# Retention and a multiplicative FFN: loads of two attention units moved ahead of weight pieces, four weight pieces converted one at a time, and the fifth unit's products moved ahead of a block's second step

## The chip, the cores and the metric

The kernel runs on one core of a Trainium2 chip. The core has five engines that take their instructions in order, each from its own queue: TensorE (PE, matrix products and transposes), VectorE (DVE), ScalarE (ACT), GpSimd (POOL) and SyncE (SP, which here only issues transfers). Transfers run on 16 DMA engines beside them. The metric is the time of one execution on the device in microseconds (us), lower is better.

## The reference

```python
# q, k, v: (B, H, S, D) = (8, 8, 576, 64)
scores = scale * np.matmul(q, k.transpose(0, 1, 3, 2))
Dmat = np.where(rel >= 0, gamma[:, None, None] ** rel[None, :, :], 0.0)
ret = scores * Dmat[None, :, :, :]
attn = np.matmul(ret, v)
x = attn.transpose(0, 2, 1, 3).reshape(B * S, H * D)   # 4608 tokens x 512
a = x @ w1                                             # 512 x 1024
b = x @ w2                                             # 512 x 1024
h = a * b @ w3                                         # 1024 x 1024
out = h @ w_out                                        # 1024 x 512
```

The attention is a causal product of scores with a decay that depends on the head and on the distance of the two positions. Its output is the input of a feed-forward part, in which two products of x are multiplied element by element. `w3` and `w_out` are multiplied with each other first, since nothing stands between them. q, k and v are float32. The four weights are float64, and the kernel turns them into float32 itself.

## The kernel before, in words

**Attention in units.** Two batches and 64 or 128 positions make a unit. The 576 positions of the first pair of batches are units 0 (64 positions) to 4 (128 each). The later pairs follow much later and are not touched by the change. One unit `g` goes through these steps:

- `load(g, names)` (L138 to L147): SP issues one transfer per name. Each is 512 KB (256 KB for unit 0). Two buffers per name hold the units, so unit 2's k waits until unit 0's k is no longer read.
- `scale(g, "q")` and `scale(g, "v")` (L256 to L266): multiply by the decay. v goes to POOL (L265), q to DVE (L265) for units 0 and 1, and to ACT in eight instructions (L263) for later ones; unit 4's v goes to ACT also.
- `front(g, "k")` or `"q"` (L268 to L283): 8 transposes on PE into two PSUM banks (L279), and two copies on ACT (L282).
- `score(g)` (L285 to L300): 16 products (L294) into four banks, then four maskings on DVE into `pm` (L297).
- `state(g)` (L302 to L322): the running k-v state: 16 products (L317) and a copy on ACT (L321).
- `pv_state(g)` and `pv(g)` (L326 to L380): products of the state with q (L336) and of the masked scores with v (L363) in two banks. The function that `pv` returns copies the result into the token tiles `xT` on ACT (L370).

**Weights in pieces.** `load_block` (L395) has SP issue one piece of 512 KB of a float64 weight, as one transfer (L406) or two (L409). There are five buffers, `raw`. `conversion` (L500) turns a piece into float32: `begin_block` gets the exponent `e` and the mantissa `m`, `end_block` puts sign and exponent together (L474) and multiplies (L485). The exponent comes from ACT in three instructions (L456, L457, L458), or, for the numbers listed in L450, from DVE in one (L452) and ACT in two (L454, L458). DVE makes the mantissa (L460, L463). `conversion` is a generator that goes forward one step for each `convert(1)`. The list in L506 holds the pieces at which the next one is not begun before the one at hand is ended. Pieces 0 to 3 are the first quarter of w1 and w2; each later four make the next quarter.

**The up products.** A block of tokens has 384 rows: 192 of each of two batches. `plain(0, 0, 0, w)` (L625) multiplies the first block with the first quarter of w1 (w=0) or w2 (w=1), in 16 products (L638) whose first eight need one piece and whose last eight the next. For w=0, ACT copies the result (L643). For w=1, DVE multiplies it in (L645). All later steps are `up(i, n, fp)` (L567), by Strassen's scheme: seven groups of four products (L585), sums of weights (`strassen_weights`, L203), sums of tokens (`strassen_tokens`, L556), five additions on DVE (L590), copies on ACT (L598, L613) and a multiplication (L619). Between them, `convert` steps and functions from the list `aside` are placed. `up(0, 1, 0)` is the second block's first step, `up(0, 0, 1)` the first block's second.

**What sets the order.** It is written out by hand, from L815 on: each engine runs its part of this program in the order in which it is written. PSUM banks for all this are seven (`acc`), handed out in turn. `keep_busy(n)` (L181) puts `n` products without use on PE.

Of the kernel before, what the change touches and what calls it, by code (L numbers as in the profile page):

```python
# [42 lines left out]
def kernel(  # L43
# [13 lines left out]
    nc = tc.nc  # L57
# [80 lines left out]
    def load(g, names, engine=nc.sync, tag=None):  # L138
        i, c = divmod(g, NC)
        sz = sizes[c]  # L140
        src = {"k": k, "q": q, "v": v}
        for nm in names:
            t = pools["ld"].tile([P, 2 * H, D], F32, tag=tag or "ld_" + nm, name="ld_" + nm,
                                 bufs=3 if tag else 2 if g < NC else 1)
            engine.dma_start(
                t[:sz], src[nm][2 * i:2 * i + 2, :, starts[c]:starts[c] + sz, :].rearrange("b h p d -> p (b h) d"))
            live[nm, g] = t  # L147
# [33 lines left out]
    def keep_busy(n):  # L181

        t = acc.tile([P, P], F32, tag="acc", name="idle")
        for _ in range(n):
            nc.tensor.matmul(t, ident, ident, start=True, stop=True)
# [70 lines left out]
    def scale(g, nm, scalar=False, engine=nc.gpsimd):  # L256
        c = g % NC
        sz = sizes[c]
        t, gam = live[nm, g], {"q": gq, "v": gk}[nm]
        t = t[:sz].rearrange("p (b h) d -> p b h d", b=2)  # L260
        if scalar:
            for h in range(H):
                nc.scalar.mul(t[:, :, h, :], t[:, :, h, :], gam[:sz, c, h:h + 1])  # L263
            return
        engine.tensor_tensor(  # L265
            out=t, in0=t, in1=gam[:sz, c].unsqueeze(1).unsqueeze(3).to_broadcast([sz, 2, H, D]), op=ALU.mult)  # L266

    def front(g, names="kq"):  # L268
        c = g % NC
        sz = sizes[c]  # L270
        for nm in names:
            src = live[nm, g]
            dst = pools["fr"].tile([P, 2, NP, P], F32, tag=nm + "T", name=nm + "T",
                                   bufs=1 if nm == "k" and g >= NC else 2)
            for b in range(2):
                tp = acc.tile([P, NP, P], F32, tag="acc", name="tp")
                for p in range(NP):
                    h = b * H + 2 * p
                    nc.tensor.transpose(tp[:, p, :sz],  # L279
                                        src[:sz, h:h + 2, :].rearrange("p a d -> p (a d)"),  # L280
                                        ident[:sz, :sz])
                nc.scalar.copy(dst[:, b, :, :sz], tp[:, :, :sz])  # L282
            live[nm + "T", g] = dst  # L283
# [18 lines left out]
    def state(g):  # L302
        c = g % NC
        sz = sizes[c]
        if c == NC - 1:
            return
        vs = live["v", g]
        kn = live["k", g]
        if c == 0:
            live["st"] = st_ps.tile([P, 2, NP, D], F32, tag="st", name="st")  # L310
        st = live["st"]

        for b in range(2):
            for p in range(NP):
                for j, hs in enumerate(heads):
                    h = b * H + 2 * p + j
                    nc.tensor.matmul(st[hs, b, p, :], kn[:sz, h, :], vs[:sz, h, :],  # L317
                                     start=(c == 0 and b == 0 and p == 0), stop=(c == NC - 2),
                                     skip_group_check=True)
        sb = pools["fr"].tile([P, 2, NP, D], F32, tag="sb", name="sb", bufs=2 if g < NC else 1)  # L320
        nc.scalar.copy(sb, st)  # L321
        live["sb", g + 1] = sb  # L322
# [72 lines left out]
    def load_block():  # L395
        n = loaded[0]
        if n == len(blocks):
            return
        key, w = blocks[n]
        t = raw.tile([P, CV, 2], I32, tag="raw", name="raw", bufs=5)  # L400
        if key[0] == "w12":
            _, fp, _, r = key
            t2 = t.rearrange("p (c n) t -> p c n t", c=2)
            src = w[2 * r * P:2 * (r + 1) * P, fp * QC:(fp + 1) * QC]
            if r == 0:
                nc.sync.dma_start(t2, src.rearrange("(c p) n t -> p c n t", p=P))  # L406
            else:
                for half in range(2):
                    nc.sync.dma_start(t2[heads[half]],  # L409
                                      src.rearrange("(c a d) n t -> a d c n t", a=2, d=D)[1 - half])  # L410
        elif key[0] == "wo":
            src = w.rearrange("(a i x) n t -> i a x n t", i=KF, x=BL)[key[1]]
            for a in range(QP):
                nc.sync.dma_start(t[a * BL:(a + 1) * BL], src[a])
        else:
            _, ft, h = key
            src = w[ft * P:(ft + 1) * P].rearrange("(j r) (a h f) t -> h a r j f t", r=BL, a=QP, h=DF // CV)
            for a in range(QP):
                nc.sync.dma_start(t[a * BL:(a + 1) * BL].rearrange("p (j f) t -> p j f t", j=P // BL), src[h, a])
        live["raw", n] = t  # L420
        loaded[0] += 1
# [13 lines left out]
    def begin_block():  # L435
        n = begun[0]
        t = live["raw", n]
        lo, hi = t[:, :, 0], t[:, :, 1]
        top = t.rearrange("p n t -> p (n t)").bitcast(BF16).rearrange("p (n u) -> p n u", u=4)[:, :, 3]
        e = raw.tile([P, CV], I32, tag="exp", name="e")  # L440
        m = raw.tile([P, CV], I32, tag="man", name="m")
        vec = nc.vector

        half = e.bitcast(BF16).rearrange("p (n u) -> p n u", u=2)[:, :, 1]
        func = mybir.ActivationFunctionType
        if n in (1, 2, 3, 2 * NQ - 1):  # L450

            vec.tensor_scalar(out=e, in0=hi, scalar1=1, scalar2=21,  # L452
                              op0=ALU.logical_shift_left, op1=ALU.logical_shift_right)
            nc.scalar.activation(e, e, func.Relu, bias=lim[:, 0:1], scale=-1.0)  # L454
        else:
            nc.scalar.activation(half, top, func.Abs)  # L456
            nc.scalar.activation(e, half.bitcast(U16), func.Relu, bias=lim[:, 0:1], scale=-1.0 / 16.0)  # L457
        nc.scalar.activation(e, e, func.Relu, bias=lim[:, 1:2], scale=-2.0 ** 23)  # L458

        vec.tensor_scalar(out=m, in0=hi, scalar1=0x000FFFFF, scalar2=0x00100000,  # L460
                          op0=ALU.bitwise_and, op1=ALU.bitwise_or)
        yield
        vec.scalar_tensor_tensor(m.bitcast(F32), in0=lo.bitcast(U32), scalar=2.0 ** -32, in1=m,  # L463
                                 op0=ALU.mult, op1=ALU.add)
        live["em", n] = e, m
        begun[0] += 1
        yield
# [32 lines left out]
    def conversion():  # L500

        yield from begin_block()
        while converted[0] < len(blocks):
            if begun[0] < len(blocks) and converted[0] not in (0, 3, 4, 6, 7):  # L506
                yield from begin_block()
            yield from end_block()
            if begun[0] == converted[0] < len(blocks):
                yield from begin_block()  # L510
# [11 lines left out]
    def convert(n):  # L522

        for _ in range(n):
            if go_on() is not None:
                return
# [286 lines left out]


    load(0, "v")  # L815
    load(1, "kq")
    load_block()
    load(1, "v")
    for _ in range(3):
        load_block()  # L820
    scale(0, "q", engine=nc.vector)
    front(0, "k")
# [1 line left out]
    front(0, "q")  # L824
    score(0)
    scale(0, "v")
    state(0)
    front(1, "k")
    pv(0)()
    scale(1, "q", engine=nc.vector)  # L830
    load(2, "kqv")
    load_block()
    keep_busy(3)
    front(1, "q")
    convert(2)
    score(1)
    scale(1, "v")
    pv_state(1)
    convert_up_to(1)
    pv(1)()  # L840
    convert(2)
    state(1)
    load(3, "kqv")
    convert_up_to(2)
    load_block()
    convert_up_to(3)
    load_block()
    plain(0, 0, 0, 0)
    front(2, "k")
    convert_up_to(4)  # L850
    load_block()
    plain(0, 0, 0, 1)
    scale(2, "q", True)
    scale(2, "v")
    front(2, "q")
    convert(2)
    score(2)
    convert_up_to(5)
    state(2)
    load(4, "kq")  # L860
    scale(3, "q", True)
    list(strassen_weights(0))
    front(3, "k")
    copies = pv(2)
    scale(3, "v")
    copies()
    front(3, "q")
    load(4, "v")
    list(strassen_tokens(0, 0, nc.vector))
    state(3)  # L870
    score(3)
    pv(3)()
    list(strassen_tokens(0, 1, nc.vector))
    convert_up_to(6)
    aside.extend([lambda: scale(4, "q", True), lambda: None, lambda: front(4, "k"), lambda: front(4, "q")])
    up(0, 1, 0, conv=2, tail=False)
    owed.append(2)
    while ("S", 1) not in live:
        convert(1)
    score(4)  # L880
    aside.append(lambda: scale(4, "v", True))
    up(0, 0, 1, conv=2, tail=False)
    owed.append(2)
    pv(4)()
    up(0, 1, 1, conv=[2, 1, 0, 2, 2], tail=False)
    owed.append(2)
    up(0, 0, 2, conv=[2, 1, 1, 2, 2], tail=False)
# [509 lines left out]
```

## Time and profile before

| What | Value |
|---|---|
| median of 3 runs | 819.23 us (818.91 to 821.7) |
| the profiled execution | 820.0 us |
| its span | 818.3 us |
| granted clock, mean of the span | 0.998 |
| DMA | 115.34 MB, mean 141 GB/s |

The stretches of 20 us show where the engines are busy. The columns are the stretch, its length, then PE, PEld (weight loads of PE), DVE, ACT and POOL busy with the number of instructions, the granted clock, the busy share of a DMA engine, and GB/s.

```profile
0.00:20.00 20.00, 16.91 (x239) 15.28 (x239) 7.95 (x18) 8.08 (x15) 3.17 (x9) 1.00 1.04 179
20.00:40.00 20.00, 18.05 (x161) 17.44 (x163) 13.13 (x21) 11.53 (x24) 3.47 (x2) 0.91 1.07 210
40.00:60.00 20.00, 19.62 (x296) 17.39 (x293) 17.82 (x29) 14.13 (x32) 2.37 (x1) 1.00 1.08 224
60.00:80.00 20.00, 18.47 (x161) 17.03 (x161) 19.79 (x38) 15.50 (x33) 0.00 (x0) 1.00 0.48 118
80.00:100.00 20.00, 20.00 (x144) 19.83 (x144) 18.60 (x33) 12.15 (x20) 1.40 (x1) 1.00 0.40 104
```

The first four stretches hold units 0 to 4, the first pieces and the first steps of `up`. A product in float32 appears as two records, so that 16 products are "x32". The end of a product is modelled, so a busy PE can hide short waits.

### The profile page before, as it was taken

To read this page: it belongs to the slowest core of one execution; us is meant where nothing else is said; L and a number is where in the kernel's file an instruction comes from. 1 tells how busy PE (TensorE), PEld (TensorE's weight loads), DVE (VectorE), ACT (ScalarE), POOL (GpSimd) and SP (SyncE) were. 2 spreads that over 40 slices of the span, in tenths; PEclk is the share of its full clock that TensorE was granted. 3 is DMA by queue.
4 is the path that set the end of the run, shared out by engine and by line. 5 is a ranking of instruction groups with operands and counts; after the bars stand their busy time and mean duration, and the time that the engine had idled before them with its cause. 6 is when DMAs were issued, how large, how long until landed. Compare 5 with 4: busy or idle time off the path is not lost.

```text
span 818.3 us, 14501 instructions
## 1 busy us (share of the span) xinstructions
PE 805.2 (98%) x5679; PEld 696.7 (85%) x5679; DVE 526.5 (64%) x787; ACT 243.3 (30%) x439; POOL 219.6 (27%) x148
## 2 busy tenths in 40 slices
PE   8999999999999999999999999999999999999998
PEld 7888999744788999888888888888888888888887
DVE  4699999997446585766545766555575656455633
ACT  3677546675110112113222111233211112232100
POOL 1110020000100503205657014167541213464300
PEclk9999999999999999999999999999999999999999
DMA  9994355569227966756964775458646612442011
GB/s 180 212 219 126 80 105 140 134 163 312 42 57 117 233 178 172 233 144 160 224 161 137 168 139 116 80 154 225 175 173 126 115 52 71 138 171 98 0 52 52
DMA packets 224036, 115.34 MB, mean 141 GB/s; under 512 B 195672, under 2 KB 207192, under 8 KB 223968
## 3 DMA queue, kind: packets, MB, share of 16 engines
q1 hardware_dynamic: 171584, 93.40, 45.1%
q10 hardware_dynamic: 52384, 21.01, 11.8%
q8 instruction: 45, 0.74, 0.4%
q14 instruction: 23, 0.19, 0.1%
HBM read 92.09 MB, written 22.28 MB: 140 GB/s over the span
## 4 chain that ended last, share of the span: by engine, by line
PE 80%; DVE 9%; DMA 4%; SPq 3%; issue 2%; ACT 1%; POOL 0%; ACTq 0%; DVEq 0%
PE up L1059 27%; PE po L754 23%; PE up L585 9%; PE ps L536 6%; PE upz L1059 4%; PE xps L363 3%; PE sc L294 3%; DMA ld_v<-in_v_dram 2%; PE st L317 1%; PE up L638 1%; DMA bl_q<-in_q_dram 1%; PE xps L336 1%; DVE room L203 1%; DVE room L590 1%; SPq L896 1%
## 5 line engine op out<-in xcount | busy, mean ns | idle before, releaser
L1082 DVE TENSOR_TENSOR room<-up,room 128x512 f32<-128x512 f32 (+1 forms) x168 | 129.1, 784 | 104.4 <-PE up L1059 101.8
L585 PE MATMUL up<-room 128*128 128x192 f32 x808 | 135.5, 328 | 2.0 <-DVE room L590 1.8
L585 PEld LDWEIGHTS up<-room 128*128 128x128 f32 x808 | 131.1, 190 | 5.0 <-DVE room L590 2.6
L754 PE MATMUL po<-w3o,room 128*128 128x256 f32 x544 | 124.1, 382 | 1.5 <-DVE ot L758 1.5
L1059 PE MATMUL up<-room,form 128*128 128x256 f32 x528 | 125.2, 379 | 0.0
L754 PEld LDWEIGHTS po<-w3o,room 128*128 128x128 f32 x544 | 102.0, 190 | 17.7 <-DVE ot L758 2.6
L1059 PE MATMUL up<-room 128*128 128x256 f32 x480 | 114.4, 379 | 0.0
L1059 PEld LDWEIGHTS up<-room,form 128*128 128x128 f32 x528 | 100.3, 190 | 13.6
L1082 POOL TENSOR_TENSOR room<-ring,room 128x512 f32<-128x512 f32 (+1 forms) x60 | 81.7, 1378 | 84.1 <-ACT ring L1081 84.1
L1059 PEld LDWEIGHTS up<-room 128*128 128x128 f32 x480 | 91.2, 190 | 12.4
L265 POOL TENSOR_TENSOR ld_v<-ld_v,gk 128x1024 f32<-128x1024 f32 (+1 forms) x19 | 39.6, 2086 | 227.9 <-DMA ld_v<-in_v_dram 91.7
L758 DVE TENSOR_TENSOR ot<-po,ot 128x256 f32<-128x256 f32 x90 | 37.7, 419 | 49.5 <-PE po L754 48.5
L754 PE MATMUL po<-wB,forms 128*128 128x256 f32 x288 | 67.5, 382 | 0.0
L590 DVE TENSOR_TENSOR room<-up,room 128x384 f32<-128x384 f32 x75 | 41.4, 552 | 33.1 <-PE up L585 32.3
L754 PEld LDWEIGHTS po<-wB,forms 128*128 128x128 f32 x288 | 54.0, 190 | 7.9 <-PE xps L363 0.5
L536 PE MATMUL ps<-wo,w3T 128*128 128x512 f32 x128 | 55.4, 594 | 0.6 <-DVE w3T L489 0.6
L243 POOL TENSOR_TENSOR bl_q<-bl_q,gqs 128x512 f32<-128x512 f32 (+1 forms) x26 | 28.3, 1107 | 94.2 <-DMA bl_q<-in_q_dram 94.2
L536 PEld LDWEIGHTS ps<-wo,w3T 128*128 128x128 f32 x128 | 24.2, 190 | 31.3 <-issue 28.9
L297 DVE TENSOR_TENSOR pm<-sc,mask 128x512 f32<-128x512 f32 (+1 forms) x72 | 42.5, 652 | 4.5 <-PE sc L294 4.5
L1116 POOL TENSOR_TENSOR room<-room 128x1024 f32<-128x1024 f32 x18 | 42.4, 2358 | 1.6 <-DVE room L1082 1.6
L1081 ACT COPY ring<-up 128x512 f32<-128x512 f32 x24 | 14.1, 586 | 89.3 <-PE up L1059 89.3
L774 ACT COPY ot<-po 128x256 f32<-128x256 f32 x18 | 6.7, 372 | 107.7 <-PE po L754 73.9
(110 smaller groups left out, 983.3 us busy)
## 6 DMA issues: line engine op xcount, KB each, us to landing
form<-kept SPq DMA_DIRECT2D x22, 896.0 KB, 5.0
room<-kept SPq DMA_DIRECT2D x20, 896.0 KB, 5.2
raw<-in_moe_w_dram SPq DMA_DIRECT2D x64, 128.0 KB, 3.0
out_dram<-ot ACTq DMA_DIRECT2D x28, 256.0 KB, 2.1
kept<-form SPq DMA_DIRECT2D x8, 896.0 KB, 5.6
bl_q<-in_q_dram SPq DMA_DIRECT2D x216, 32.0 KB, 2.5
ld_v<-in_v_dram ACTq DMA_DIRECT2D x12, 512.0 KB, 7.4
bl_k<-in_k_dram SPq DMA_DIRECT2D x160, 32.0 KB, 2.9
```

The source lines that it names most:

```text
L243: nc.gpsimd.tensor_tensor(out=part, in0=part, in1=gqs[:, :, n0:n0 + n].unsqueeze(3).to_broadcast([P, NP, n, BL]), op=ALU.mult)
L265: engine.tensor_tensor(out=t, in0=t, in1=gam[:sz, c].unsqueeze(1).unsqueeze(3).to_broadcast([sz, 2, H, D]), op=ALU.mult)
L294: nc.tensor.matmul(sc[j][:sz, p, :sz], kT[hs, b, p, :sz], qT[hs, b, p, :sz], start=True, stop=True)
L297: nc.vector.tensor_mul(pm[:sz, b, j, :, :sz], sc[j][:sz, :, :sz], mask[:sz, :sz].unsqueeze(1).to_broadcast([sz, NP, sz]))
L536: nc.tensor.matmul(ps, live["w3T", ft][:, g, :], live["wo"][:, g, :], start=(g == 0), stop=(g == KF - 1))
L585: nc.tensor.matmul(ps[:, w, :], a[:, w, r, :], b[:, r, :], start=(new and w == r == 0), stop=(w == r == 1), skip_group_check=True)
L590: nc.vector.tensor_add(c[:, to], ps, c[:, sb])
L754: nc.tensor.matmul(ps[nm], a[A][:, f // 2, f % 2, :], live["W"][B][:, f, :], start=(f == 0 and not on), stop=(f == NP - 1), skip_group_che ...
L758: nc.vector.tensor_add(ot[:, to[0], to[1]], ps[nm], ot[:, sb[0], sb[1]])
L1059: nc.tensor.matmul(ps[:, w, :], a[:, w, :], b, start=(pr in (1, 5) and w == 0), stop=True, skip_group_check=True)
L1082: engine.tensor_tensor(out=at(out, l), in0=spread(got), in1=at(old if first and old is not None else out, l), op=ALU.add)
L1116: return lambda: engine.tensor_tensor(out=slab[:, h, p], in0=slab[:, h, p], in1=slab[:, h + 1, p], op=ALU.mult)
```

## The change

Three things are moved, in the hand-written order and in the two lists of `conversion`:

- Unit 1's q, k and v are issued together, ahead of piece 0. Unit 3's are issued ahead of piece 4, which before was issued ahead of them; pieces 5 and 6 now follow piece 4 at once. In both units q is issued ahead of k.
- Pieces 1, 2 and 3 are each begun when the one before is ended, and the exponents of pieces 2 and 3 come from ACT alone. Piece 4 is converted after score 3 rather than around score 2. The two transposes of unit 2 stand behind both `plain` calls, the weight sums of the first quarter ahead of score 2's maskings, and score 3 ahead of state 3.
- Score 4, the scaling of v4 and `pv(4)` stand ahead of `up(0, 0, 1)`; before, `pv(4)` stood behind it.

The three fillers of `keep_busy(3)` are dropped. Nothing else differs from piece 8 on.

```diff
-        if n in (1, 2, 3, 2 * NQ - 1):
+        if n in (1, 2 * NQ - 1):
...
-            if begun[0] < len(blocks) and converted[0] not in (0, 3, 4, 6, 7):
+            if begun[0] < len(blocks) and converted[0] not in (0, 1, 2, 3, 4, 6, 7):
...
     load(0, "v")
-    load(1, "kq")
-    load_block()
-    load(1, "v")
-    for _ in range(3):
+    load(1, "qkv")
+    for _ in range(4):
         load_block()
...
     scale(0, "v")
+    scale(1, "q", engine=nc.vector)
     state(0)
+    pv(0)()
+    load(2, "kqv")
+    front(1, "q")
     front(1, "k")
-    pv(0)()
-    scale(1, "q", engine=nc.vector)
-    load(2, "kqv")
-    load_block()
-    keep_busy(3)
-    front(1, "q")
-    convert(2)
     score(1)
     scale(1, "v")
+    convert(2)
     pv_state(1)
     convert_up_to(1)
     pv(1)()
     convert(2)
     state(1)
-    load(3, "kqv")
+    load(3, "qkv")
+    load_block()
+    load_block()
     convert_up_to(2)
     load_block()
     convert_up_to(3)
     load_block()
     plain(0, 0, 0, 0)
+    convert_up_to(4)
+    scale(2, "q", True)
+    plain(0, 0, 0, 1)
     front(2, "k")
-    convert_up_to(4)
-    load_block()
-    plain(0, 0, 0, 1)
-    scale(2, "q", True)
     scale(2, "v")
+    list(strassen_weights(0))
     front(2, "q")
-    convert(2)
     score(2)
-    convert_up_to(5)
+    list(strassen_tokens(0, 0, nc.vector))
     state(2)
     load(4, "kq")
     scale(3, "q", True)
-    list(strassen_weights(0))
     front(3, "k")
     copies = pv(2)
     scale(3, "v")
     copies()
     front(3, "q")
     load(4, "v")
-    list(strassen_tokens(0, 0, nc.vector))
+    score(3)
     state(3)
-    score(3)
+    convert_up_to(5)
     pv(3)()
...
     up(0, 1, 0, conv=2, tail=False)
     owed.append(2)
+    scale(4, "v", True)
+    score(4)
     while ("S", 1) not in live:
         convert(1)
-    score(4)
-    aside.append(lambda: scale(4, "v", True))
+    pv(4)()
     up(0, 0, 1, conv=2, tail=False)
     owed.append(2)
-    pv(4)()
     up(0, 1, 1, conv=[2, 1, 0, 2, 2], tail=False)
```

## The prediction

> **What bounds the kernel now.** I read the page's first line and the busy shares, then windows of 20 us, then the timelines of PE, DVE, ACT and SP over the first 130 us, the landings of the single loads, and the waits. The page says that TensorE carries the kernel:
>
> ```profile
> span 818.3 us, 14501 instructions
> PE 805.2 (98%) x5679; PEld 696.7 (85%) x5679; DVE 526.5 (64%) x787; ACT 243.3 (30%) x439; POOL 219.6 (27%) x148
> ```
>
> From 82.00 to 810.00 us PE is busy for 725.07 of 728.00 us, and the change touches nothing there. So a change in the first 80 us counts only by the moment at which PE gets through it. There PE does have waits. Its timeline (start, length, products, and the idle time before with its releaser):
>
> ```profile
> 18.22 1.10 PE L336 MATMUL xps<-qT,sb 64*64 64x128 f32 x32
> 21.62 3.53 PE L363 MATMUL xps<-pm,ld_v 128*64 128x128 f32 x32 [2.30 <-POOL ld_v L265]
> 26.02 5.79 PE L638 MATMUL up<-room 128*128 128x192 f32 x32
> ...
> 39.00 2.06 PE L294 MATMUL sc<-qT,kT 64*128 64x128 f32 x32 [0.24 <-ACT qT L282]
> ...
> 51.24 2.65 PE L363 MATMUL xps<-pm,ld_v 128*64 128x128 f32 x32
> 54.14 5.69 PE L585 MATMUL up<-room 128*128 128x192 f32 x32 [0.24 <-ACT room L370]
> ...
> 65.75 2.06 PE L294 MATMUL sc<-qT,kT 64*128 64x128 f32 x32
> 67.73 8.07 PE L585 MATMUL up<-room 128*128 128x192 f32 x48
> 77.33 1.57 PE L585 MATMUL up<-room 128*128 128x192 f32 x8 [1.53 <-DVE room L590]
> ```
>
> The reader should see three things. Unit 1's value product (L363 at 21.62) waits 2.30 us for v1, which the chain of waits shows landing at 19.60. It then takes 3.53 us where its sisters take 1.97. And 1.53 us are lost before 77.33, where DVE is late. VectorE's timeline says why:
>
> ```profile
> 16.31 0.43 DVE L460 TENSOR_SCALAR m<-raw 128x512 int32<-128x512 int32 x1 [1.48 <-DMA raw<-in_moe_w_dram]
> 27.41 0.69 DVE L474 SCALAR_TENSOR_TENSOR e<-raw,e 128x512 int32<-128x512 int32 x1 [1.76 <-ACT e L458]
> 36.70 0.56 DVE L645 TENSOR_TENSOR room<-up,room 128x384 f32<-128x384 f32 x1 [3.69 <-PE up L638]
> ...
> 70.21 2.48 DVE L297 TENSOR_TENSOR pm<-sc,mask 128x512 f32<-128x512 f32 x4
> ```
>
> Piece 0 lands at 16.3. DVE idles up to 38, and from 54.40 to 80 it has no gap. Unit 4's masking (70.21) comes 2.5 us after its scores ended at 67.73.
>
> **Loads, and piece 0.** SP now issues q1, k1, v1 and then the pieces. Before, the order was k1, q1, piece 0, v1. These loads share the engines (210 GB/s from 5 to 25 us) and landed at 11.5, 13.5, 16.3 and 19.6. I give the places their times: q1 11.5, k1 13.5, v1 16.3. Piece 0 takes the next place. It lands at the earliest at 18.3 (2.0 us for 512 KB at the 259 GB/s of 10 to 15 us) and at the latest at v1's 19.6. I take 19.0, nearer to the only row for that place. Pieces 1 to 3 and unit 2 keep their places. Unit 3's three loads pass piece 4, which is wanted only near 50 us.
>
> With v1 scaled by POOL (1.90) at 18.3, and scores 1 at about 15.5, L363 runs from 18.5 to 20.5 and state 1 to 21.6, against 26.1. That gain of 4.5 us does not reach the end: the next products are L638's, and they need pieces.
>
> **The pieces one by one.** Per piece ACT takes 2.3 us (16.56 to 18.87), or 1.5 where DVE makes the exponent (0.34, L452). L474 and L485 take 1.4.
> - Piece 0: 19.0 + 2.3 + 1.4 = 22.7. L638's first half starts there, so PE has idled from 21.6.
> - Piece 1: + 0.34 + 1.5 + 1.4 = 26.0. The second half (8 products at 0.33) runs to 28.65.
> - Piece 2: behind the state copy (0.57) ACT ends at 27.4, so it is ready at 28.8.
> - Piece 3: its activations now stand on ACT behind both L643 copies, which need the products that end at 28.65. 29.35 + 2.3 + 1.4 = 33.05. The last half of L638 runs to 35.7, with PE idle from 31.45.
> - Then unit 2's two transposes (0.87 each) and the 1.28 us from q's transpose to its scores (37.72 to 39.00): scores 2 start at 35.7 + 0.87 + 1.28 = 37.85, against 39.00. **-1.15 us.**
>
> The two L452 less on DVE (0.84) and one activation more on ACT for each of pieces 2 and 3 (0.75) are in this. The three removed fillers (0.94) lay in time that PE now spends waiting, so they are worth nothing by themselves.
>
> **Units 2 and 3.** DVE's weight sums collided with POOL's scaling of v3 before (1.4 us each for two of them, 0.70 alone). Now v3 lands near 40, after them, so masking 2 keeps the 1.15. Score 3 ahead of state 3 lets masking 3 start earlier, and the 0.68 us by which L363 at 51.24 was stretched goes. In its place score 3 waits 0.7 for the q copies, which stand on ACT behind eight scalings (2.45), two k copies and two evictions, and state 3 no longer fills that gap. L585 starts near 53.0, -1.1. Its second product needs the token sums, though, and these now stand on DVE behind piece 4, whose activations stand behind state 3's copy: 49.65 + 0.6 + 2.25 + 1.4 = 53.9, against 54.40. **What is left is -0.5.** Without piece 4 in that place it would be -1.1.
>
> **Unit 4's products ahead of the second step.** DVE's work from the token sums to masking 4 is the same list, instruction by instruction, and has no gap. So masking 4 comes when it came, less 0.5. In the old times: scores end at 67.73, L336 takes 1.03, then L363 waits for the first two maskings (71.4), runs 0.95, waits for the fourth (72.65), and ends at 73.6. The 28 products follow at 0.3255 (52 in 16.90 us from 88.37), to 82.7. Before, PE had the same work done at 81.77. **+0.95**: the added wait of 2.9 us is bigger than the 1.53 that goes. All 28 products stand behind it on PE, and DVE, which waits for them, falls idle near 73 to 76. v4's scaling on ACT is now ready near 70.5, just in time. The piece loads on SP move with DVE. POOL's first token sum of the third block moves from 83.31 to about 74.5. There it no longer stretches L460 (1.11 against 0.42), which is off the path.
>
> **Sum.** -0.5 + 0.95 = +0.45 on the profiled execution's 820.0 (span 818.3 and 1.7 around it): 820.45. The median of the runs shown is 819.23, 0.8 lower, and I add the 0.45 to it: **819.7**, with 818.6 to 820.8 for this case (piece 0 at 18.3 or 19.6: -0.7, +0.6, and as much for the rest).
>
> **The clock.** PE's idle time has a price beyond itself. Windows of the clock's 3.41 us:
>
> ```profile
> 18.01:21.42 3.41, 1.31 (x38) 0.95 (x34) 3.41 (x5) 0.83 (x2) 1.75 (x1) 1.00 0.93 243
> 21.42:24.83 3.41, 3.21 (x30) 3.21 (x32) 3.34 (x7) 0.00 (x0) 0.15 (x1) 0.51 1.13 204
> ...
> 76.03:79.40 3.37, 2.06 (x28) 1.84 (x32) 3.33 (x7) 2.23 (x3) 0.00 (x0) 1.00 0.69 155
> ```
>
> The second column is PE's busy time, the third from the end the granted clock. A window 38% busy was followed by one at half clock. One 61% busy was not. The changed kernel's window from 69.20 to 72.61 is about 47% busy by my times, in between. If it counts as idle, PE loses half of 3.41, 1.7 us. I take none and keep 1.7 as the other end. The Trainium skill ("TensorE: Matmul & The Clock Gate", Part 1) puts the half clock after an idle window of about 3.4 us and calls the window free-running. By that, no wait of 2.9 us costs anything. The row above speaks against it, with 2.1 us of idle time in the window.
>
> **Rivals.**
> - *Slower: half clock behind unit 4's wait.* For it: the 38% row. Against: the 61% row. It decides once less than about half of one window is busy. 819.7 + 1.7 = **821.4**.
> - *Slower: pieces land later still*, since three 512 KB loads go ahead of them and share the engines. One more us on piece 0 goes through the whole chain, and part of it may meet the clock: **821.0**.
> - *Faster: masking 4 is not late.* If DVE works off its list earlier than I have it, the lead of 1.1 at L585 stays and the 1.53 before 77.33 goes: **816.6**. Against: DVE has no gap from 54.40 to 80.
> - *The change doesn't do what it says*: v1 lands no earlier, because loads in flight overlap. L363 stays near 21 and still ends before piece 1 is ready: 819.7 again.
>
> **Numbers.** The forecast (with the last rival) 0.50, half clock 0.20, late pieces 0.13, faster 0.17. The range is 816.2 to 822.6: the faster case with 0.4 of its own, and half clock with 1.2 for late pieces beside it. A measurement can tell about 0.5% (4.1 us) from no change. All the lost time found above (2.30, 1.56 and 0.68 of L363, 0.94 of fillers, 1.53) is 7.0 us, so faster by that much needs most of it to go: 0.05. Slower by that much needs half clock more than once: 0.09. Within 0.5%: 0.86.
>
> **What would show it.** Right: L363 of unit 1 near 18.5; L638 in pieces from 22.7 to 35.7; scores 2 near 37.9; L585 near 53, its second product waiting for DVE; L363 of unit 4 waiting over 2 us for DVE's masking; no wait of 1.5 us for L590. Wrong: piece 0 outside 18.3 to 19.6, a granted clock of 0.5 after 60 us, masking 4 before 69 us, or a difference after 130 us other than at 83 us.

## The result, and the profile after

The changed kernel took **823.91 us** (median of 8 executions, 822.08 to 828.2), the kernel before 819.3 us (8 executions, 818.07 to 821.7). The ratio is 1.0063, with a 95% interval of 1.0039 to 1.0088. The same kernel measured once more, on another occasion, gave 1.0085 [1.0055, 1.0114]. So the change costs 5 to 7 us, where I had forecast 0.45 us and a range up to 822.6.

The execution shown here is the longest of the eight: 828.2 us, with a span of 826.3 us. The repeat's profile (experiment 1) is of an execution of 824.81 us. I name both where they differ. First the page's span and busy shares:

```profile
span 826.3 us, 14493 instructions
PE 807.6 (98%) x5673; PEld 698.5 (85%) x5673; DVE 527.4 (64%) x785; ACT 245.0 (30%) x441; POOL 216.4 (26%) x148
```

Busy time hardly says anything: PE is 2.4 us busier with six records fewer, since the full clock began late in this execution (10.6 us after the start, before 4.4) and the first products took longer. DVE and ACT are within 2 us of before. The span is 8.0 us longer, so most of the loss is idle time. PE's timeline has it (start, length, products, and the idle time before with its releaser):

```profile
20.64 1.97 PE L363 MATMUL xps<-pm,ld_v 128*64 128x128 f32 x32
...
24.27 2.84 PE L638 MATMUL up<-room 128*128 128x192 f32 x16 [0.72 <-DVE room L485]
...
36.20 2.87 PE L638 MATMUL up<-room 128*128 128x192 f32 x16 [3.13 <-DVE room L485]
...
41.16 2.06 PE L294 MATMUL sc<-qT,kT 64*128 64x128 f32 x32 [0.34 <-ACT qT L282]
...
56.66 5.84 PE L585 MATMUL up<-room 128*128 128x192 f32 x32 [0.25 <-ACT room L370]
...
70.41 1.10 PE L336 MATMUL xps<-qT,sb 64*64 64x128 f32 x32
73.66 0.40 PE L363 MATMUL xps<-pm,ld_v 128*64 128x128 f32 x2 [2.15 <-ACT ld_v L263]
74.30 3.06 PE L363 MATMUL xps<-pm,ld_v 128*64 128x128 f32 x30 [0.24 <-DVE pm L297]
77.29 15.32 PE L585 MATMUL up<-room 128*128 128x192 f32 x88
...
95.65 4.66 PE L585 MATMUL up<-room 128*128 128x192 f32 x27 [0.43 <-DVE room L590]
```

The reader is to see three things against the lines of before. The wait for v1 ahead of unit 1's L363 is gone, as meant. The first L638 group comes earlier than before, but the last quarter of L638 now waits 3.13 us for a piece, and scores 2 start at 41.16 (before 39.00). Unit 4's L363 waits 2.15 us for v4's scaling and 0.24 for the masking, and then its 30 records take 3.06 us (the same 30 take 2.19 in run 5, at full clock). The wait of 1.53 us for L590 is gone, and one of 0.43 us has come in a later group.

Why L363 is longer is told by the windows of the clock (columns as above: the second is PE's busy time, the third from the end the granted clock). The first two lines are the changed kernel's, the last two the repeat's:

```profile
72.04:75.45 3.41, 1.54 (x20) 1.12 (x20) 3.41 (x7) 1.65 (x6) 0.00 (x0) 1.00 0.00 0
75.45:78.87 3.42, 3.42 (x19) 3.09 (x20) 0.84 (x2) 1.07 (x2) 0.75 (x1) 0.50 0.00 0
...
68.15:71.57 3.42, 1.54 (x42) 1.18 (x38) 3.38 (x7) 3.39 (x10) 0.00 (x0) 1.00 0.15 58
71.57:74.98 3.41, 3.13 (x26) 2.81 (x28) 2.91 (x6) 0.31 (x2) 0.00 (x0) 0.50 0.00 0
```

A window in which PE was busy for 1.54 of 3.41 us (45%) is followed by one at half clock. It costs about 1.6 us: L363's 30 records take 0.87 us more than in run 5, and the 88 records of L585 behind them take 15.32 us instead of 14.57.

Why the last quarter of L638 is late is on ACT and DVE. First ACT's timeline, then DVE's, then POOL's:

```profile
20.36 0.79 ACT L456 ACTIVATE e<-raw 128x512 bf16<-128x512 bf16 x1 [2.30 <-DMA raw<-in_moe_w_dram]
...
30.44 0.48 ACT L643 COPY room<-up 128x384 f32<-128x384 f32 x1 [0.82 <-PE up L638]
30.82 0.79 ACT L456 ACTIVATE e<-raw 128x512 bf16<-128x512 bf16 x1
```

```profile
33.88 2.27 DVE L485 SCALAR_TENSOR_TENSOR room<-m,e 128x512 f32<-128x512 f32 x1
```

```profile
33.67 1.93 POOL L265 TENSOR_TENSOR ld_v<-ld_v,gk 128x1024 f32<-128x1024 f32 x1 [15.92 <-DMA ld_v<-in_v_dram]
```

Piece 0 is there at 20.36 (16.3 before). Piece 3's first activation, at 30.82, stands behind both L643 copies, which themselves need products of piece 1. And in this execution piece 3's last step (L485) takes 2.27 us instead of 0.69, because POOL scales v2 beside it. In the repeat, POOL began at 33.78 and L485 at 33.66: there POOL took 2.34 instead of 1.90 and L485 the usual 0.69, so the wait ahead of L638 was 1.56 and scores 2 started at 39.37.

### The profile page after: what moved, and what is told of

It is laid out like the page before. It is cut to its first block, busy times and chain, and to the rows that moved or that the text cites. A ratio compares the mean times of both kernels' runs of the same rounds, so it can differ in the third digit from the quotient of the medians.

```text
span 826.3 us, 14493 instructions
## 1 busy us (share of the span) xinstructions
PE 807.6 (98%) x5673; PEld 698.5 (85%) x5673; DVE 527.4 (64%) x785; ACT 245.0 (30%) x441; POOL 216.4 (26%) x148
## 4 chain that ended last, share of the span: by engine, by line
PE 75%; DVE 8%; DMA 6%; SPq 5%; ACT 3%; issue 2%; ACTq 0%; DVEq 0%
PE up L1055 26%; PE po L754 22%; PE up L585 7%; PE ps L536 6%; PE upz L1055 4%; PE xps L363 3%; PE sc L294 3%; SPq L228 2%; DMA bl_q<-in_q_dram 2%; PE st L317 1%; DMA kept<-form 1%; SPq L145 1%; DMA raw<-in_moe_w_dram 1%; DVE room L590 1%; DVE e L474 1%
## 5 line engine op out<-in xcount | busy, mean ns | idle before, releaser
L585 PE MATMUL up<-room 128*128 128x192 f32 x808 | 136.0, 329 | 1.1 <-DVE room L590 0.7
L585 PEld LDWEIGHTS up<-room 128*128 128x128 f32 x808 | 131.9, 191 | 4.1 <-DVE room L590 1.5
L754 PE MATMUL po<-w3o,room 128*128 128x256 f32 x544 | 124.2, 382 | 3.0 <-DVE ot L758 3.0
L754 PEld LDWEIGHTS po<-w3o,room 128*128 128x128 f32 x544 | 102.0, 190 | 19.4 <-DVE ot L758 4.5
L754 PE MATMUL po<-wB,forms 128*128 128x256 f32 x288 | 67.5, 382 | 0.0
L590 DVE TENSOR_TENSOR room<-up,room 128x384 f32<-128x384 f32 x75 | 41.5, 553 | 36.2 <-PE up L585 35.1
L754 PEld LDWEIGHTS po<-wB,forms 128*128 128x128 f32 x288 | 54.0, 190 | 7.9 <-PE xps L363 0.5
L779 DVE TENSOR_TENSOR room<-room,forms 128x512 f32<-128x512 f32 x17 | 13.7, 808 | 41.8 <-PE po L754 41.8
```

Of the source, the lines that this page charges most:

```text
L585: nc.tensor.matmul(ps[:, w, :], a[:, w, r, :], b[:, r, :], start=(new and w == r == 0), stop=(w == r == 1), skip_group_check=True)
L590: nc.vector.tensor_add(c[:, to], ps, c[:, sb])
L754: nc.tensor.matmul(ps[nm], a[A][:, f // 2, f % 2, :], live["W"][B][:, f, :], start=(f == 0 and not on), stop=(f == NP - 1), skip_group_che ...
```

## The experiments

Fourteen runs, in four groups. Those of one group share a chip and the executions of the kernel before. Differences in us are the ratio less one, times 820. "Full clock" counts the executions whose mean granted clock was 0.999 or more: one window at half clock makes it 0.998. The kernel before had full clock in 72 of 105 executions, with a mean of 819.53 us, and 820.63 in the other 33.

| Run | Ratio, 95% interval | us | Full clock |
|---|---|---|---|
| the changed kernel | 1.0063 [1.0039, 1.0088] | +5.2 | 3 of 8 |
| 1 the changed kernel again | 1.0085 [1.0055, 1.0114] | +7.0 | 0 of 6 |
| 2 unit 4 as before | 1.0039 [1.002, 1.0058] | +3.2 | 8 of 12 |
| 3 before, unit 4 moved | 1.0033 [1.0017, 1.0049] | +2.7 | 1 of 12 |
| 4 before, unit 1's loads | 1.0009 [0.9994, 1.0024] | +0.7 | 9 of 12 |
| 5 fillers in unit 4's wait | 1.0044 [1.0027, 1.006] | +3.6 | 6 of 7 |
| 6 lists as before | 1.0039 [1.0026, 1.0051] | +3.2 | 1 of 12 |
| 7 piece 0 ahead of v1 | 1.0076 [1.0054, 1.0097] | +6.2 | 2 of 6 |
| 8 before, delayed | 1.001 [0.9998, 1.0023] | +0.8 | 6 of 11 |
| 9 lists and unit 4 as before | 1.0005 [0.9994, 1.0017] | +0.4 | 12 of 12 |
| 10 lists as before, fillers | 1.0013 [1.0001, 1.0026] | +1.1 | 12 of 12 |
| 11 before, lists | 1.0033 [1.0019, 1.0046] | +2.7 | 2 of 12 |
| 12 exponents as before | 1.0052 [1.0033, 1.0072] | +4.3 | 1 of 6 |
| 13 before, score 4 late | 0.999 [0.9979, 1.0] | -0.8 | 11 of 12 |
| 14 changed and mended, score 4 late | 0.9991 [0.9981, 1.0002] | -0.7 | 12 of 12 |

**Theory 1**: there are two losses, late pieces in the first 40 us, and unit 4's wait with a half clock behind it. **Theory 2**: only unit 4's move costs, and the late first part of the profile was chance, since the clock's record began late in it.

**1. The changed kernel again.** No edit.

> The changed kernel itself once more, for a second profile beside the first, whose execution took 828.2 us where the median of 8 was 823.9. Both theories: about 823.9 us, 4.6 over before. In the trace, theory 1 (two losses: late pieces, and unit 4's wait with half clock behind it) expects L585 to start at 55.5 to 57 us (54.14 before) and half clock for 3.41 us after L363 of unit 4 waited. Theory 2 (only unit 4's move costs; the first profile's late start of the scores, 11.9 against 9.3 us, was chance of the clock and made the rest of its delay) expects L585 near 53.5 when the clock is full from 5 us on.

It was 7.0 us slower, at the upper end of what the first measurement allowed. Its profile has the half clock from 71.57 to 74.98. L585 starts at 54.71, between the 55.5 to 57 of theory 1 and the 53.5 of theory 2. Its last L638 group and its scores 2 in PE's timeline:

```profile
34.41 2.87 PE L638 MATMUL up<-room 128*128 128x192 f32 x16 [1.56 <-DVE room L485]
...
39.37 2.06 PE L294 MATMUL sc<-qT,kT 64*128 64x128 f32 x32 [0.34 <-ACT qT L282]
```

**2. Unit 4 put back.**

```diff
-    scale(4, "v", True)
-    score(4)
     while ("S", 1) not in live:
         convert(1)
-    pv(4)()
+    score(4)
+    aside.append(lambda: scale(4, "v", True))
     up(0, 0, 1, conv=2, tail=False)
     owed.append(2)
+    pv(4)()
```

> The changed kernel with unit 4's scores, scaling and products back behind the first block's second step. Theory 1: the 2.7 us of this part go, the late pieces' 2.0 to 2.7 stay: 821.2 us. Theory 2: 819.3, as before.

+3.2 us is left with unit 4 as before. Theory 2, which gave it nothing, falls. Theory 1 had about 1.9 us for what is left, 1.3 too little.

**3. Only unit 4 moved.** The same lines the other way round, in the kernel before.

> The kernel before with only unit 4's scores, scaling and products moved ahead of the first block's second step. By the prediction's own terms 819.3 + 0.95 = 820.3. Theory 1: 2.7 with the half clock, 822.0. Theory 2: all of the 4.6, 823.9.

+2.7 us: theory 1's number, and not the prediction's 0.95. Eleven of twelve executions were below full clock. The one that was profiled had full clock, and there the same wait of 2.16 us at L363 fell across the border of two windows: PE was busy for 2.01 us of the one and 2.41 us of the other, and no half clock followed:

```profile
65.40:68.81 3.41, 2.01 (x50) 1.65 (x47) 3.38 (x7) 3.35 (x9) 0.00 (x0) 1.00 0.37 120
```

**4. Only unit 1's loads.**

```diff
-    load(1, "kq")
-    load_block()
-    load(1, "v")
-    for _ in range(3):
+    load(1, "qkv")
+    for _ in range(4):
         load_block()
```

> The kernel before with only unit 1's loads changed: q, k, v, then four pieces. Theory 1: piece 0 lands 3 to 4 us later and the pieces' chain starts so much later, of which L638 had 3.4 us of cover by the late v1 (it started at 26.02 and its second half waited for piece 1 anyway): 1 to 2 us slower, 820.3 to 821.3. Theory 2: no difference, 819.3. In the trace v1 lands near 16 and piece 0 near 20 by both.

+0.7 us, with an interval from -0.5 to 2.0, which holds both theories. Piece 0 was late (20.17) in this run too, so a late piece 0 together with an early v1 costs little where the lists are as before.

Next I asked what the half clock and the parts of the first 40 us cost. **Theory 1a**: ACT's chain of activations, one piece after the other, makes the first part late. **Theory 1b**: it is the pieces' landing. **Theory 3**: the clock has no price of its own. **Theory 4**: a delay is paid once more between 250 and 350 us.

**5. Six fillers in unit 4's wait.** They do nothing but keep PE busy.

```diff
+    pv_state(4)
+    keep_busy(6)
     pv(4)()
```

> The changed kernel with six fillers (0.31 us each) on TensorE between unit 4's state products (L336) and its value products (L363), in the 2.15 us in which it waited. The changed kernel took 4.6 to 6.9 us more than the one before so far. Theory 1 (the wait has a second price, the half clock behind it): no window at half clock after 60 us, and 1.2 to 1.7 us less than that, so 3.2 to 5.5 us over before. Theory 3 (only the wait itself and VectorE behind it count): half clock or not, 4.6 to 6.9 us over before.

+3.6 us, and full clock in 6 of 7 executions, against 3 of 14 without fillers. The time is below the 4.6 to 6.9 of theory 3, though its interval reaches up to 4.9. Run 10 settles it. PE's timeline shows that L363 starts when it did, with the fillers where PE was idle:

```profile
72.06 1.60 PE L185 MATMUL idle<-ident 128*128 128x128 f32 x12 [0.30 <-DVE room L590]
73.91 0.40 PE L363 MATMUL xps<-pm,ld_v 128*64 128x128 f32 x2 [0.24 <-issue]
74.55 2.19 PE L363 MATMUL xps<-pm,ld_v 128*64 128x128 f32 x30 [0.24 <-DVE pm L297]
```

The 30 records of L363 take 2.19 us here and 3.06 in the changed kernel.

**6. The lists as before.**

```diff
-        if n in (1, 2 * NQ - 1):
+        if n in (1, 2, 3, 2 * NQ - 1):
...
-            if begun[0] < len(blocks) and converted[0] not in (0, 1, 2, 3, 4, 6, 7):
+            if begun[0] < len(blocks) and converted[0] not in (0, 3, 4, 6, 7):
```

> The changed kernel with the two lists of the conversion as they were before: pieces 1 and 2 begun while the piece ahead of them is still at hand, exponents of pieces 2 and 3 from VectorE. Theory 1a (the first part is late because ACT makes three activations for each piece, one piece after the other): scores 2 start 1 us or more earlier than the 39.3 to 41.2 us of the changed kernel, and the time is 1 to 2 us below its 4.6 to 6.9 us over before. Theory 1b (it is late because the pieces land late): within 0.5 us of the changed kernel.

+3.2 us, 2.0 to 3.8 below the changed kernel, more than theory 1a's 1 to 2. Scores 2 start at 37.23 us, 2.1 before the repeat's. Not all of this is the lists' doing: ACT could begin on piece 0 at 18.79 here and at 20.16 in the repeat, although SP issued its load at 10.67 and 10.70:

```profile
18.79 0.80 ACT L456 ACTIVATE e<-raw 128x512 bf16<-128x512 bf16 x1 [3.28 <-DMA raw<-in_moe_w_dram]
```

```profile
20.16 0.80 ACT L456 ACTIVATE e<-raw 128x512 bf16<-128x512 bf16 x1 [3.86 <-DMA raw<-in_moe_w_dram]
```

From piece 0 to scores 2 it is 18.44 us here and 19.21 in the repeat. So theory 1a holds by the time, and by 0.8 us in the trace.

**7. Piece 0 ahead of v1 again.**

```diff
-    load(1, "qkv")
-    for _ in range(4):
+    load(1, "qk")
+    load_block()
+    load(1, "v")
+    for _ in range(3):
         load_block()
```

> The changed kernel with piece 0 issued ahead of v1 again. Theory 1b (pieces land late): piece 0 lands near 18.3 us in place of 20.2, scores 2 start 1 to 1.9 us earlier, and the time is 1 to 1.9 us below the 4.6 to 6.9 us over before. Theory 1a (ACT's chain of activations): scores 2 start at most 0.5 us earlier, and the time is the changed kernel's within 0.5 us.

+6.2 us: the changed kernel's time. Theory 1b falls, and plainly, since piece 0 now came four us earlier. ACT's timeline, then PE's:

```profile
16.00 0.78 ACT L456 ACTIVATE e<-raw 128x512 bf16<-128x512 bf16 x1
```

```profile
21.48 1.97 PE L363 MATMUL xps<-pm,ld_v 128*64 128x128 f32 x32 [2.73 <-POOL ld_v L265]
...
34.38 2.87 PE L638 MATMUL up<-room 128*128 128x192 f32 x16 [1.55 <-DVE room L485]
```

Now v1 takes the late place, L363 waits 2.73 us for it, and the copies of its result (L370) stand on ACT ahead of piece 1's activations, which start at 24.24 (24.28 in the repeat). The last L638 group waits as before. Which of the two loads is late does not matter in these runs.

**8. The kernel before, delayed.** Four products without use ahead of the first product of the first block's third step. They ran at 89.91 us, not near the 126.7 us that the expectation names.

```diff
+                for _ in range(delay.pop() if delay and (i, n, fp) == (0, 0, 2) else 0):
+                    nc.tensor.matmul(ps[:, 0, :P], ident, ident, start=True, stop=True, skip_group_check=True)
```

> The kernel before, with four products without use (128x128, 0.31 us each, 1.25 us together) ahead of the first product of the first block's third step, near 126.7 us, where TensorE had 0.26 us of idle time. Nothing else differs. Theory 4 (a shift of TensorE by about 1 us changes which of VectorE's and POOL's instructions fall on each other between 250 and 350 us, and costs more there): 1.5 to 3 us over before, with TensorE waits at L754 that the profile of before lacks. Theory 1 alone (what is lost early is lost once): 1.0 to 1.25 us over before.

+0.8 us for 1.05 us of products (x8 in PE's timeline), with an interval from -0.2 to 1.9. Theory 4 (1.5 to 3 us) is not borne out, though its lower end is not excluded: a delay is paid about once.

**9. Lists and unit 4 as before.** The edits of runs 2 and 6 together. What is left is the loads, the order of units 1 to 3, piece 4 behind score 3, and the dropped fillers.

> The changed kernel with the two lists of the conversion and unit 4's steps as before. What is left of the change: the loads of units 1 and 3 ahead of pieces, the order of the steps of units 1 to 3, piece 4 behind score 3, no fillers. Theory 1 (the lists and unit 4 are the whole loss; +2.3 to +3.4 and +2.6 to +3.7 us of the 4.6 to 6.9): the second block's first step starts near 52.4 us (54.1 in the profile of before), and the time is from 1.5 us under to 0.5 us over before. Theory 5 (the loads and the order cost too): 0.7 to 2 us over before.

+0.4 us. Theory 1 holds by the time: the lists and unit 4 are nearly the whole loss. Its sign in the trace did not come: the second block's first step starts at 53.98, not near 52.4, with piece 0 at 20.23 and scores 2 at 38.63. PE's timeline shows L638 without its last wait:

```profile
24.12 2.84 PE L638 MATMUL up<-room 128*128 128x192 f32 x16 [0.47 <-DVE room L485]
28.25 8.29 PE L638 MATMUL up<-room 128*128 128x192 f32 x48 [1.29 <-DVE room L485]
```

The first group starts 0.15 us before that of the changed kernel's profile, and the last one ends at 36.5 instead of 39.1.

**10. Lists as before, and the fillers.** The edits of runs 5 and 6 together.

> The changed kernel with the lists as before, and six fillers in unit 4's wait. The kernel with the lists alone put back took 3.45 us more than the one before, and none of its 12 runs had a full clock. Theory 1 (1.4 us for each window at half clock, and the rest is unit 4's wait): most runs at a clock of 1.0, and 1.5 to 2.2 us over before. Theory 3 (no price of the clock): 3 to 3.5 us over before.

+1.1 us, below theory 1's 1.5 to 2.2, and all executions at full clock. Theory 3 falls. Without the fillers (run 6) it was +3.2, with one of twelve at full clock (0.999, which the expectation counted as below). So the half clock that follows unit 4's wait is worth about 2 us, and the wait itself, by the difference to run 9, 0.7 us, which the two intervals do not tell from nothing.

**11. Only the lists.** The lists of the changed kernel, in the kernel before.

> The kernel before with only the two lists changed: pieces 1 to 3 begun one by one, exponents of pieces 2 and 3 from ACT alone. Theory 1a: 1.5 to 2.5 us over before, L638 waits for L485 of piece 3. Rival (the lists cost only where unit 2's loads and the late start of piece 0 stand with them): 0 to 0.7 us over before.

+2.7 us, just above theory 1a's range. Theory 1a holds without the late loads. PE's timeline, then ACT's:

```profile
37.40 2.87 PE L638 MATMUL up<-room 128*128 128x192 f32 x16 [2.67 <-DVE room L485]
```

```profile
31.29 0.48 ACT L643 COPY room<-up 128x384 f32<-128x384 f32 x1 [0.82 <-PE up L638]
31.73 1.07 ACT L282 COPY kT<-tp 128x512 f32<-128x512 f32 x2
32.69 0.79 ACT L456 ACTIVATE e<-raw 128x512 bf16<-128x512 bf16 x1
```

Piece 3's three activations stand behind the L643 copies, and here behind unit 2's copies also. L638 waits 2.67 us, of which 0.9 is a collision: POOL scales v2 from 34.17 on, and L474 of piece 3 takes 1.60 us instead of 0.69. Two of the twelve executions had full clock, with a mean of 820.04 us; the other ten had 822.86. The profiled one is of the ten, and its half clock lies where before has it, behind unit 1's wait for v1, which this kernel keeps:

```profile
19.14:22.55 3.41, 1.18 (x26) 1.16 (x24) 3.38 (x5) 0.00 (x0) 1.90 (x1) 1.00 0.91 229
22.55:25.96 3.41, 3.41 (x49) 3.29 (x46) 1.43 (x4) 2.30 (x4) 0.00 (x0) 0.50 1.21 166
```

**12. Only the exponents as before.** The first half of run 6's edit.

> The changed kernel with the exponents of pieces 2 and 3 from VectorE again, but the pieces still begun one by one. If ACT's three activations are the price of the lists: 2 to 2.5 us less than the changed kernel, so 2.5 to 4.5 us over before, and scores 2 start near 37.5 us where the first piece is ready at 22.6. If it is the beginning one by one: at most 0.7 us less than the changed kernel.

+4.3 us, but its interval (2.7 to 5.9) reaches far into the changed kernel's, so the times do not tell the two lists apart. In the profile, scores 2 start 14.76 us after the first L638, against 15.31 in the repeat and 14.53 with both lists back. By that row, ACT's extra activations are 0.55 us of this chain's 0.78, and the beginning one by one is 0.2. The later first group (24.06 in the repeat, 22.70 in run 6) is no part of the lists' price: piece 0 was there at 20.16 and at 18.79, and its load is issued ahead of all that the lists order. What the lists add now and then is the collision of v2's scaling with piece 3's L485, which the later piece 3 brings about: 1.6 us in the profiles of the changed kernel and of run 5, none in runs 1 and 2.

**13 and 14. Score 4 the other way.** If DVE's list is what holds PE near 77 us (theory 6), unit 4's masking should move behind the step, not ahead of it. Run 13 is the kernel before with this edit, run 14 is run 9 with it.

```diff
-    score(4)
-    aside.append(lambda: scale(4, "v", True))
+    aside.extend([lambda: scale(4, "v", True), lambda: None, lambda: None, lambda: None, lambda: score(4)])
     up(0, 0, 1, conv=2, tail=False)
     owed.append(2)
-    pv(4)()
+    aside.extend([lambda: None, lambda: pv(4)()])
     up(0, 1, 1, conv=[2, 1, 0, 2, 2], tail=False)
```

> The kernel before with unit 4 moved the other way: score 4, and with it VectorE's masking, to the end of the first block's second step, and unit 4's products into the step after it. Theory 6 (VectorE's unbroken list from 54 to 80 us sets the time there, and masking 4 is what makes it late): the 1.53 us of idle time at L590 near 77 us is gone, and the time is 0.5 to 1.5 us under before. Rival (VectorE is late whatever stands where): a wait of the same size comes back within the next step, 0.3 us under to 0.5 us over before.

> The changed kernel's loads and order for units 1 to 3, with the two lists as before, and unit 4 moved the other way as in the run beside it. The same without that move took 0.4 us more than before. Theory 6: 0.2 to 1.2 us under before. Rival: 0 to 1 us over before.

-0.8 us [-1.7, 0.0] and -0.7 us [-1.6, 0.2]. PE's timeline of run 13:

```profile
67.31 6.74 PE L585 MATMUL up<-room 128*128 128x192 f32 x40 [0.32 <-DVE room L203]
74.82 1.57 PE L585 MATMUL up<-room 128*128 128x192 f32 x8 [0.77 <-DVE room L590]
```

The wait for L590 is halved, from 1.53 to 0.77 us, and 0.32 us comes in for weight sums that DVE has not finished. The result lies between theory 6 and its rival: the masking was part of DVE's lateness, not all of it. These two are the fastest kernels of the study, at the edge of what can be told from before. Run 14 against run 9 is 1.1 us.

## Why the prediction was wrong

Runs 9, 10, 5 and 1 make a ladder from the kernel before to the changed one. Loads and order: +0.4. Unit 4's products moved, with the clock kept up: +0.7. The lists: +2.5. The half clock behind unit 4's wait: +1.6 to +3.4. My terms were -0.5 for loads, lists and order together, +0.95 for unit 4, and none for the clock.

So two steps failed: the gain of 1.15 us at scores 2, with the -0.5 that was left of it (the runs show +2.9), and the half clock taken at nothing. The first missed by 3.4 us, the second by 1.6 to 3.4. Each rung is a difference of two ratios that are known to 1 to 2.4 us. The rung of the lists has a second witness, the executions at full clock alone, each run against its own kernel before: run 5 is 3.5 us over, run 10 1.3, run 2 2.5, run 9 1.0. So the lists cost 2.2 us (run 5 less run 10) or 1.5 (run 2 less run 9) without any half clock.

- **Loads, and piece 0: late by 1.2 to 1.4 us in the two profiles, and not what decided.** POOL scaled v1 from 15.85 us on (17.29 in the repeat; I had 16.3 for its landing). L363 ran at 20.64 and 19.25 (I had 18.5), and its wait was nothing and 0.30 us. Piece 0 came at 20.36 and 20.16, above my latest bound of 19.6. SP issued it at 10.78 us, the place that v1 had before (10.88). In the other runs with these loads it came at 18.79, 19.05 and 19.29 (runs 6, 14, 10) and at 20.06 to 20.54 (runs 2, 4, 5, 9, 12). So one place in the queue has a spread of 1.8 us, and my bounds came from one row. Run 7, with piece 0 at 16.00 and v1 late in its place, was no faster.
- **The pieces one by one: the first step that failed.** The chain itself was nearly right. From piece 0's landing to scores 2 I had 18.85 us. Runs 1 and 2 took 19.21; the changed kernel's first profile took 20.80 and run 5 20.88, with the collision of v2's scaling and L485 (1.58 us), which I had not looked for in this place. I had gone over v3's collision with the weight sums only, and that one did come back in the first profile (v3 was scaled at 41.52 and the four sums took 4.44 us), though PE did not wait for it. What failed is "-1.15 us", the comparison with before, in two ways. With the lists as before the same stretch takes 18.40 to 18.44 us (runs 6, 9, 10, 14): the lists make it longer by 0.8 us, or by 2.4 with the collision. I had seen that piece 3's activations stand behind both L643 copies, and priced it. I had not set it against what the lists did before, where piece 3 was ready as soon as L638 wanted it. And I set my chain against the 39.00 of one profile. The same code up to that point gave 38.87 in run 13, 37.48 in run 3 and 37.30 in run 8. PE's timeline of run 13, then of run 8:

```profile
21.49 3.59 PE L363 MATMUL xps<-pm,ld_v 128*64 128x128 f32 x32 [2.36 <-POOL ld_v L265]
...
38.87 2.06 PE L294 MATMUL sc<-qT,kT 64*128 64x128 f32 x32 [0.24 <-ACT qT L282]
```

```profile
20.97 1.97 PE L363 MATMUL xps<-pm,ld_v 128*64 128x128 f32 x32 [1.71 <-POOL ld_v L265]
...
37.30 2.06 PE L294 MATMUL sc<-qT,kT 64*128 64x128 f32 x32 [0.24 <-ACT qT L282]
```

The two late ones, 39.00 and 38.87, are executions with the half clock over this L363 (3.53 and 3.59 us); the two early ones have full clock (1.97). My own window at 0.51 from 21.42 to 24.83 shows it, but I counted its absence as a gain and added the sum to the median of before, whose executions mostly have full clock (72 of 105). On the mean of the four, before is at 38.16. The changed order gave 41.16, 39.37, 39.27, 41.42 and 39.33 (the changed kernel and runs 1, 2, 5, 7), 40.11 on the mean. That is +1.95 where I had -1.15.
- **Units 2 and 3.** The smaller readings came true: L363 of unit 3 is back at 1.97 us, score 3 waits 0.46 for the q copies (I had 0.7), and the token sums behind piece 4 delay L585's second product by 0.50 us in run 6. The lead of 1.1 us that they were to be taken from did not exist.
- **Unit 4's products ahead of the second step: right in size, with another releaser.** The wait was 2.39 us (I had 2.9), and the move costs 0.7 us by run 10 against run 9 (I had 0.95). The wait's releaser was v4's scaling on ACT, which I had called just in time, with masking 4 only 0.24 behind it. A wait of 0.42 to 0.44 for L590 in a later group, seen in all profiles with this move, was not in my list.
- **The clock: the second step that failed.** I wrote "I take none and keep 1.7 as the other end". My window was 47% busy, between a row of 38% and one of 61%, and I gave the half clock a chance of 0.20. The window was 45% busy (1.54 of 3.41 us), and 11 of 14 executions were below full clock. The rows now lie closer together: 1.54 us busy was followed by half clock in the changed kernel and in run 1, and 1.49 in run 12, while 1.70 us (the changed kernel's window from 34.49 to 37.90), 1.82 (run 6) and 2.01 (run 3) were not. The Trainium skill ("TensorE: Matmul & The Clock Gate", Part 1) makes an idle window of about 3.4 us the condition; here 1.87 us of idle time in one window was enough, so the measurement decides against that reading. What the page says of the free-running window agrees: whether the wait falls into one window (changed kernel, runs 1 and 12) or across two (run 3) changes from one execution to the next, and so does the time. One such window costs about 1.6 us; two of run 1's six executions have a mean clock of 0.996, which is two windows, and took 829.65 us against 825.62 for the other four, more than the second window explains by itself.
- **The rivals.** Half clock and late pieces both came, together. My range allowed 1.2 us for late pieces beside the 1.7 for half clock, but the first part was off by 3.4 us (+2.9 for loads, order and lists, where I had -0.5). "Masking 4 is not late" did not come.
- **The signs of a wrong prediction** fired as listed: piece 0 outside 18.3 to 19.6, a clock of 0.5 after 60 us, and differences after 130 us.

The last needs a word. From the product that starts at 126.71 in the profile of before, all kernels issue the same instructions, and yet they took 691.6 us there, 693.5 in the changed kernel's profile and 691.9 in the repeat's. The difference lies between 250 and 360 us, where PE waits up to 1.07 us at L754. It comes from DVE instructions that fall beside POOL's scaling of v, or just miss it. DVE's timeline of before, then of the changed kernel:

```profile
340.42 0.69 DVE L779 TENSOR_TENSOR room<-room,forms 128x512 f32<-128x512 f32 x1 [4.07 <-PE po L754]
```

```profile
347.00 2.32 DVE L779 TENSOR_TENSOR room<-room,forms 128x512 f32<-128x512 f32 x1 [3.98 <-PE po L754]
```

In before, POOL's scaling began 0.12 us after this instruction, and in the changed kernel 0.13 us ahead of it. Run 8's profile took 2.2 us more than before from its product on, but its median is only 0.8 us up. So this is spread between executions, and I do not charge it to the change.

**What stays open**: where else the half clock fell in the executions below full clock of runs 2 and 11, which have no wait of unit 4. Those of run 2 averaged 825.64 us against 821.89, and its one profile had full clock. Run 11's profile has it behind unit 1's wait for v1, but ten of its twelve executions were below full clock, against six of 29 of the kernel before beside it. The waits for piece 3, 1.55 and 2.67 us, are a likely place, but that is argued and not shown. Open too is why the lists cost 2.5 us by the times, where the traces show 0.8, or 2.4 with the collision.

## What to carry to other kernels

Price an idle stretch on TensorE by the clock's window too: when a wait can leave one window less than half busy, take the half clock as the likelier case, and try a few fillers in the wait before giving up the move. Before a stage's new start is called a gain, set it against several executions of the old kernel and not one profile, and look whether that profile has a half clock that most executions lack; here that alone was 0.84 us. When an in-order engine serves a chain of pieces, look at what stands on its queue ahead of the last piece, since an earlier first piece is worth nothing if the last one waits behind copies.

## What the runs showed of the hardware

- **DVE and POOL hold each other up.** Which of the two is slowed depends on which starts first, by a tenth of a us: DVE's 0.69 us became 2.27, 2.32 and 2.37 (the last in run 5) where POOL had begun 0.21, 0.13 and 0.08 us earlier, and POOL's 1.90 became 2.34 (the repeat) and 2.33 (before) where DVE had begun 0.12 us earlier. In the first of these cases L485 ended at 36.15, 0.55 us after POOL's 35.60, as if it had waited for POOL's end. The Trainium skill ("SBUF — State Buffer", "Who interferes with whom") agrees: a DVE instruction with two inputs in SBUF contends with a POOL instruction that reads SBUF, through a shared read interface, and the order of issue decides which of the two is held up.
- **The full clock begins at different times.** Its record began at 4.30 us (run 6) to 10.85 us (run 5) after the start of the span, and where it began late the eight fillers of the start (x16) took 3.36 to 3.58 us instead of 2.05.
- **The border of the half clock is sharp.** 1.54 us busy of 3.41 was followed by it, 1.70 was not. One case does not fit: in run 4 it came for two windows in a row, from 14.91 us, behind a window that was 52% busy by the records (1.77 us).
